# Loading each piece of MLP weights in two transfers of 117 and 11 rows

## The chip, the cores and the metric

The kernel runs on one core of a Trainium2 chip. The core has TensorE (matrix multiplications), VectorE, ScalarE and GpSimd (element-wise work), SyncE (which here only issues DMAs), and 16 DMA engines that move data between HBM and the on-chip memory SBUF. The metric is the device time of one execution in microseconds; the profile's "span" is the part of it from the first to the last instruction of the program.

## What is computed

A recurrence over 768 time steps (RWKV-7, for 4 batches of 8 heads with 40 channels), whose output of 3072 tokens x 320 channels goes through an MLP with a hidden width of 2048.

```python
    for t in range(S):
        kt, vt, rt = (k[:, :, t], v[:, :, t], r[:, :, t])
        wt, at, bt = (w[:, :, t], a[:, :, t], b[:, :, t])
        y[:, :, t] = np.einsum('bhd,bhde->bhe', rt, state)
        Sa = np.einsum('bhde,bhe->bhd', state, at)
        state_decay = state * wt[:, :, None, :] - np.einsum('bhd,bhe->bhde', Sa, bt)
        state = state_decay + np.einsum('bhd,bhe->bhde', vt, kt)
...
    h = x @ w_in
    g = h * (1.0 / (1.0 + np.exp(-1.702 * h)))
    return (g @ w_out).astype(np.float32)
```

The weights w_in (320 x 2048) and w_out (2048 x 320) come as 64-bit floating-point numbers, since the setup scales them by a 64-bit factor. The kernel turns them into 32-bit numbers on the chip.

## The kernel before

**Tiling.** The sequence is cut into 12 chunks of 64 steps, and each chunk into two units of two batches, 24 units in all. For a unit, `load_w` and `load` fetch its inputs (logw, wc, ak, b, rv, RV, time), `decay` and `prep` scale them, `inverse` inverts a triangular system in five "levels" (TensorE into `ps_level`, copies by ScalarE and VectorE, transposes into `EX`), and `solve` applies the state and writes the unit's output `x`. `part_with` and `get_back` (lines 979 to 989) write x to DRAM and read it back transposed, as `xT`. After every second unit, `mlp` adds the chunk's matmuls into `ps_up` and `ps_down` (lines 995 to 1044). The recurrence hands its state from unit to unit; the MLP only needs its chunk's xT and the weights.

**Order of the work.** Nothing is scheduled by the compiler. Every piece of work is a task with a rank, a cost for each engine that may run it, and the tasks it comes after. `Plan.order` (line 105) simulates the engines with these costs and writes out one order of instructions; `refined` (line 247) shifts ranks at random and keeps what its own simulation calls shorter. Each engine then runs its instructions strictly in that order, and semaphores join the engines. SyncE is one such queue: a DMA that waits there holds up all those behind it. The DMAs share eight semaphores in turn, so that each DMA also waits until the one eight places before it has landed.

**The weights.** They are kept in one tile `w_sb` for the whole kernel. `weights` (line 505) loads them in eight pieces, four of w_in and four of w_out, of 128 rows x 1280 numbers of 64 bits, or 1280 KB. Each piece goes through `weight` (line 462): one DMA (line 498) puts the 64-bit numbers in a place that is free at the time (the spare tile `extra`, a part of `w_sb` that is not filled yet, or the buffers of `xT`, as the list `raws` says). Then ScalarE takes the upper words (`rebased`, line 478), VectorE clamps and shifts them (482, 486) and scales the lower words (490), and GpSimd adds the two (`joined`, 494). In the order that results, the first five pieces are issued between 12.9 and 17 us of the span, the sixth at 41.0, the seventh at 65.7 and the eighth at 94.2 us.

**The other DMAs.** Loads of ak, b and rv come in two DMAs of 40 rows each (line 528); logw, wc, RV and time in one of 128 rows; x goes out in two of 40 rows and comes back in two of 64; results go out in two of 64.

## Time and profile before

| | |
|---|---|
| median of 3 runs | 716.97 us (716.28 to 717.66) |
| the profiled execution | 715.64 us, span 713.9 us |
| TensorE clock granted, mean | 0.985 |
| DMA traffic | 69.81 MB in 31,860 packets, mean 98 GB/s |
| of it instruction fetches | 159 packets on q8, 21 on q14 |
| TensorE busy 12 to 50 us | 26.0 of 38 us, clock 0.78, DMA engines busy 0.88 |
| TensorE busy 50 to 80 us | 22.3 of 30 us, clock 0.93, DMA engines busy 0.53 |
| TensorE busy 80 to 110 us | 28.3 of 30 us, clock 1.00, DMA engines busy 0.36 |
| TensorE busy 110 to 714 us | 593.4 of 604 us, clock 1.00, DMA engines busy 0.27 |

The last four rows are stretches of the span. DMA engines busy is the mean over the 16 engines. In a time line each row gives the start in us from the span's beginning, the duration, engine, line, operation and tiles, how many equal instructions follow each other, and in brackets the time that the engine sat idle before it and what ended that. SPq is the queue that issues DMAs; its durations are those of the issuing alone.

### The profile page before, as it was taken

To read this page: it belongs to the slowest core of one execution; us is meant where nothing else is said; L and a number is where in the kernel's file an instruction comes from. 1 tells how busy PE (TensorE), PEld (TensorE's weight loads), DVE (VectorE), ACT (ScalarE), POOL (GpSimd) and SP (SyncE) were. 2 spreads that over 40 slices of the span, in tenths; PEclk is the share of its full clock that TensorE was granted. 3 is DMA by queue.
4 is the path that set the end of the run, shared out by engine and by line. 5 is a ranking of instruction groups with operands and counts; after the bars stand their busy time and mean duration, and the time that the engine had idled before them with its cause. 6 is when DMAs were issued, how large, how long until landed. Compare 5 with 4: busy or idle time off the path is not lost.

```text
span 713.9 us, 43522 instructions
## 1 busy us (share of the span) xinstructions
PE 673.0 (94%) x20256; PEld 562.4 (79%) x20256; DVE 423.8 (59%) x747; ACT 347.7 (49%) x683; POOL 204.6 (29%) x260
## 2 busy tenths in 40 slices
PE   4667899999999999999999999999999999999997
PEld 4566779887888788788888998779978788877563
DVE  6689777756766576577474775666675656421000
ACT  4465636656365465454555565256445535342020
POOL 5367244442431321331342233220341320200000
PEclk9879999999999999999999999999999999999999
DMA  7955351431441341341432241251341230111000
GB/s 244 394 193 181 111 168 47 139 99 44 129 121 32 113 137 32 111 139 42 120 121 86 72 124 50 83 147 33 107 115 32 81 96 5 41 49 31 20 3 19
DMA packets 31860, 69.81 MB, mean 98 GB/s; under 512 B 5056, under 2 KB 14272, under 8 KB 30656
## 3 DMA queue, kind: packets, MB, share of 16 engines
q1 hardware_dynamic: 31680, 67.03, 30.5%
q8 instruction: 159, 2.61, 1.5%
q14 instruction: 21, 0.17, 0.1%
HBM read 59.15 MB, written 7.86 MB: 94 GB/s over the span
## 4 chain that ended last, share of the span: by engine, by line
PE 88%; DVE 5%; issue 3%; DMA 2%; ACT 1%; SPq 0%; ACTq 0%; DVEq 0%
PE ps_down L330 29%; PE ps_up L330 28%; PE ps_level L330 9%; PE ps_y L330 4%; PE ps_B L330 4%; PE ps_X L330 2%; PE ps_T L330 1%; PE ps_Q L330 1%; PE ps_rz L330 1%; PE ps_A L330 1%; PE ps_RV L330 1%; PE ps_N L330 1%; PE ps_zT L330 1%; PE ps_cum L330 1%; DMA rv<-in_rv 1%
## 5 line engine op out<-in xcount | busy, mean ns | idle before, releaser
L330 PE MATMUL ps_up<-xT_all,w_sb 64*64 64x256 f32 x3840 | 251.7, 378 | 1.8 <-issue 1.7
L330 PE MATMUL ps_down<-w_sb,g 64*64 64x320 f32 x3072 | 243.0, 431 | 0.8 <-issue 0.6
L330 PEld LDWEIGHTS ps_up<-xT_all,w_sb 64*64 64x64 f32 x3840 | 157.5, 133 | 27.1 <-issue 2.7
L330 PEld LDWEIGHTS ps_down<-w_sb,g 64*64 64x64 f32 x3072 | 131.1, 133 | 45.4 <-issue 2.4
L736 ACT ACTIVATE EX<-ES,quads 128x256 f32<-128x256 f32 x124 | 56.2, 501 | 56.8 <-DVE ES L731 56.4
L1008 ACT ACTIVATE g<-ps_up 128x1024 f32<-128x1024 f32 x48 | 49.1, 1024 | 39.6 <-PE ps_up L330 39.4
L330 PEld LDWEIGHTS ps_level<-W,EX 64*64 64x64 f32 x2560 | 57.5, 134 | 8.3 <-ACT zT L878 1.0
L780 ACT COPY W<-ps_level 128x512 f32<-128x512 f32 x55 | 32.2, 586 | 55.3 <-PE ps_level L330 54.7
L657 POOL TENSOR_TENSOR kh<-time,G 128x320 f32<-128x320 f32 x23 | 20.9, 910 | 131.9 <-PE ps_y L330 70.7
L330 PE MATMUL ps_level<-W,EX 64*64 64x64 f32 (+1 forms) x2560 | 55.7, 218 | 0.9 <-ACT zT L878 0.6
L782 DVE TENSOR_TENSOR E<-two,ps_level 128x256 f32<-128x256 f32 x80 | 33.2, 415 | 39.1 <-ACT W L780 38.7
L1034 DVE TENSOR_TENSOR ob<-ob,ps_down 128x320 f32<-128x320 f32 x24 | 11.6, 482 | 59.6 <-ACT ob L1032 58.7
L726 POOL TENSOR_TENSOR PT<-two,PT 128x256 f32<-128x256 f32 x18 | 13.1, 728 | 109.8 <-DVE PT L719 105.1
L330 PE MATMUL ps_level<-PT,EX 64*64 64x64 f32 (+2 forms) x1280 | 37.5, 250 | 5.0 <-issue 4.0
L330 PEld LDWEIGHTS ps_level<-PT,EX 64*64 64x64 f32 x1280 | 35.4, 152 | 7.9 <-issue 4.9
L973 POOL TENSOR_TENSOR x<-zr,FT 128x128 f32<-128x128 f32 x80 | 40.9, 539 | 0.0
L731 DVE STREAM_TRANSPOSE ES<-E 128x256 f32<-128x256 f32 x80 | 35.6, 444 | 3.9
L911 ACT COPY B<-ps_B 128x416 f32<-128x416 f32 x38 | 19.1, 504 | 37.2 <-PE ps_B L330 36.9
L330 PE MATMUL ps_y<-RV,kh 64*64 64x104 f32 x768 | 35.7, 251 | 1.4 <-DVE M L927 1.4
L330 PE MATMUL ps_y<-M,bh 64*64 64x104 f32 x768 | 35.6, 249 | 1.2 <-issue 1.2
L649 POOL TENSOR_TENSOR ak<-ak,FT 128x512 f32<-128x512 f32 x16 | 21.5, 1345 | 50.0 <-DMA ak<-in_ak 31.0
L1032 ACT COPY ob<-ps_down 128x320 f32<-128x320 f32 x22 | 9.4, 425 | 53.1 <-PE ps_down L330 53.0
(136 smaller groups left out, 1168.1 us busy)
## 6 DMA issues: line engine op xcount, KB each, us to landing
time<-in_time SPq DMA_DIRECT2D x24, 320.0 KB
ak<-in_ak SPq DMA_DIRECT2D x48, 160.0 KB
rv<-in_rv SPq DMA_DIRECT2D x48, 160.0 KB
xT_all<-x_dram SPq DMA_DIRECT2D x48, 160.0 KB
wc<-in_wc SPq DMA_DIRECT2D x20, 264.0 KB
logw<-in_w SPq DMA_DIRECT2D x24, 160.0 KB
RV<-in_v SPq DMA_DIRECT2D x24, 160.0 KB
b<-in_b SPq DMA_DIRECT2D x48, 80.0 KB
```

The costliest lines, as they stand in the source:

```text
L330: nc.tensor.matmul(o, lhsT, rhs, start=start, stop=True, skip_group_check=True)
L649: plan.add(R, {"DVE": 690.0, "POOL": 1270.0, "sbuf": True}, lambda t: of(t.engine).tensor_mul(ahT(), ahT(), FT_of(i)), reads=T("ak", "FT") ...
L657: plan.add(R + 4, {"POOL": 870.0, "DVE": 490.0, "sbuf": True}, lambda t, n=n, dst=dst: of(t.engine).tensor_mul(dst(i)[:, :, :D], by_head(t ...
L726: plan.add(R, {"DVE": 430.0, "POOL": 750.0, "sbuf": True}, lambda t: of(t.engine).tensor_sub(at(W0_t, i)[:, :, :32], two32.unsqueeze(1).to ...
L731: plan.add(rank, dve(256), lambda t: nc.vector.transpose(ES(n), source(t)), writes=[key("ES", n, 6)], **reads)
L736: nc.scalar.activation(dst[:, :, h], ES(n), ACT.Copy, scale=quads[:, h, :1])
L780: plan.add(rank, any2(512), lambda t: copy(t.engine)(tiles_of(W(n + 1)), blocks(psum(t, ""), 64)), writes=[key("W", n + 1, 5)], pair=pair)
L782: plan.add(rank, dve(256), lambda t: nc.vector.tensor_sub(tiles_of(E(n + 1)), every(two32, [128, 2, 4, 32]), blocks(psum(t, ""), 64)[:, :, ...
L911: plan.add(R, any2(416), lambda t: copy(t.engine)(dst(), psum(t, "")[:, :, :208]), writes=[("Bv", i)] if x and c > 0 else T("B"), pair=(na ...
L973: of(t.engine).tensor_mul(x[:, b ^ u, b], both(i)[:, at, :64], FT_of(i)[:, at])
L1008: plan.add(-45, {"ACT": 1030.0, "table": "gelu"}, lambda t: nc.scalar.activation(g_of(c * NQ + q).rearrange("p m r n -> p r m n"), psum(t, ...
L1034: plan.add(-45, dve(320), lambda t: nc.vector.tensor_add(ob_of(serial), ob_of(serial), psum(t, "")[:, 1, :DM]), reads=[("ob", serial)], wr ...
```

## The change

Each of the eight pieces of weights is loaded by two DMAs in place of one: rows 0 to 116, then rows 117 to 127, into the same places. The planner's task stays one task with the same cost, so the order of tasks on every engine is the same as before. What reads a piece now waits for both DMAs, and the semaphores of all DMAs behind are handed out anew.

```diff
+    ROWS = [slice(0, 117), slice(117, 128)]
...
-        plan.add(rank, {"SP": 350.0}, lambda t: nc.sync.dma_start(raw(), src), reads=before, writes=T("wt"), size=128 * PIECE * 8)
+        def fetched(t):
+            for some in ROWS:
+                nc.sync.dma_start(raw()[some], src[some])
+        plan.add(rank, {"SP": 350.0}, fetched, reads=before, writes=T("wt"), size=128 * PIECE * 8)
```

## The prediction

> **What bounds the kernel now.** I read the page first (busy shares, slices, DMA queues), then the chain of waits for the first 150 us, the list of waits, the time lines of TensorE, ScalarE and the DMA-issuing queue, and at last the trace's own records of single DMA packets, which no view prints.

> ```profile
> PE 673.0 (94%) x20256; PEld 562.4 (79%) x20256; DVE 423.8 (59%) x747; ACT 347.7 (49%) x683; POOL 204.6 (29%) x260
> ...
> PE   4667899999999999999999999999999999999997
> ...
> PEclk9879999999999999999999999999999999999999
> DMA  7955351431441341341432241251341230111000
> ...
> q8 instruction: 159, 2.61, 1.5%
> ```

> TensorE is full from the fifth slice on, so what is to be won lies in the first 80 us or so: 713.9 - 673.0 = 40.9 us of idle TensorE, 28.6 of it (from a table of 5 us stretches) before the first MLP matmul at 79.2 us. In that time the TensorE clock also drops and the DMA engines are at their busiest. The q8 line is the key: 159 packets, 2.61 MB, so 16.4 KB a packet. It is TensorE's program, fetched while it runs.

> What TensorE waits for between 15 and 110 us, and where its time line shows it:

> ```profile
> PE ps_level L330 <- issue: 5.5, 3, 2.4
> PE ps_X L330 <- DVE T L853: 3.3, 2, 2.9
> PE ps_cumc L330 <- issue: 2.1, 1, 2.1
> PE ps_Q L330 <- POOL T L738: 1.9, 1, 1.9
> PE ps_up L330 <- issue: 1.7, 1, 1.7
> PE ps_RV L330 <- issue: 1.3, 1, 1.3
> ```

> ```profile
> 23.13 0.42 PE L330 MATMUL ps_level<-PT,ident 64*64 64x128 f32 x4 [1.55 <-issue]
> ...
> 29.80 0.77 PE L330 MATMUL ps_cumc<-edges,logw 64*64 64x65 f32 x28 [2.10 <-issue]
> ...
> 36.27 0.48 PE L330 MATMUL ps_level<-PT,EX 64*64 64x96 f32 x12 [1.56 <-issue]
> ...
> 68.26 0.45 PE L330 MATMUL ps_RV<-rv 64*64 64x64 f32 x11 [1.33 <-issue]
> ...
> 74.78 1.38 PE L330 MATMUL ps_level<-PT,EX 64*64 64x96 f32 x26 [2.43 <-issue]
> ```

> "issue" is a wait that no semaphore explains. Counted in TensorE's records, each such stop stands exactly where 256 instructions end (records 705, 961, 1217, 3009, 3265 and, at 101.44 us, 4801, all 193 modulo 256), and TensorE goes on 1.2 to 1.6 us after a 16 KB packet of q8 has ended. So these six stops, 1.55 + 2.10 + 1.56 + 1.33 + 2.43 + 1.74 = 10.7 us, are waits for the program. The packet itself takes 0.9 to 1.4 us everywhere; what differs is its start after TensorE enters the block before: mostly 0.1 to 2.1 us, but 3.98, 4.33, 3.76, 3.97 and 4.27 us for blocks entered at 16.9, 23.1, 29.8, 68.3 and 94.9 us. Those are the times at which weights move:

> ```profile
> 12.91 0.33 SPq L498 DMA_DIRECT2D extra<-in_w_in  x1
> 13.40 0.81 SPq L498 DMA_DIRECT2D w_sb<-in_w_in  x2
> ...
> 65.65 0.35 SPq L498 DMA_DIRECT2D extra<-in_w_out  x1
> ...
> 94.15 0.35 SPq L498 DMA_DIRECT2D extra<-in_w_out  x1
> ```

> A piece is 1280 KB, 128 rows of 10,240 bytes; a row takes 0.39 us in the packet records, so 8 rows on each of 16 engines are 3.1 us, just the delay of a fetch. The fetch stands behind the weights' share of one DMA engine.

> The chain of waits (start, us, what) holds five of the six; the one at 66.8 us is not on it:

> ```profile
> 21.58 1.55 issue
> ...
> 72.35 2.43 issue
> ...
> 99.71 1.74 issue
> ```

> [...]packets of the 40-row loads (4,096 bytes) run ten at a time and hardly ever more.[...]

> **The change part by part.**
> (1) Eight more DMAs on the sync queue, 0.35 us each to issue. Every DMA there waits for the landing of the one eight places earlier, so the halves use up places: unit 2's b (issued at 17.6 and 20.7 us) will wait for the third piece, unit 2's ak (27.8) for the fourth, its second half of rv (32.5) for the fifth. With the slower pieces below I get about 28, 32 to 34 and 37 us. First uses are at 45.5 (POOL, ak), 47.2 (VectorE, b) and 52.4 us (TensorE, rv): covered by 8 us or more, also if the work comes 4 us sooner. Cost 0; without that cover up to 3 us.

> (2) A piece takes 10 rows x 0.39 = 3.9 us[...] instead of 3.1. The first five pieces ended at 19.4, 22.7, 26.1, 30.1 and 35.4 us; each falls 0.8 us further behind: about 20.3, 24.3, 28.5, 33.3 and 39. Their readers on ScalarE:

> ```profile
> 20.68 1.39 ACT L478 ACTIVATE w_sb<-extra 128x1280 f32<-128x1280 f32 x1
> 26.28 0.80 ACT L813 COPY PT<-ps_level 128x768 f32<-128x768 f32 x1 [4.21 <-PE ps_level L330]
> ```

> The first piece is read at once, so ScalarE will stand about 0.9 us with the copy of ps_level queued behind it, but it sits 4.2 us before that copy anyway. The others are read at 35.0, 36.4, 38.7 and 45.6 us, 5 us or more after landing, except the fifth if the work moves up by more than 5 us. Cost 0, at worst 2. The sixth and later pieces lose a tail instead: in the eighth, one engine ran on alone from 100.9 to 102.8 us, and ScalarE waited 1.0 us for it.

> (3) [...]If the fetch queue lies on one of them, a fetch starts about 1 us after its block is entered, lands 3.4 us after it (1.1 + 1.0 + 1.3), and nearly every block before 80 us takes TensorE longer than that. Which engine it is the trace does not print. It shows one thing: in the fetch at 234.1 us (0.94 us long) packets of 4,096 bytes fill 9.6 us, ten whole engines, so the fetch is on none of those ten[...].[...]I take 0.69 for a free one.

> What the stops are then worth, by what is late next. First stop: the next level needs VectorE's EX, ready at 22.3 us, against 24.1 when it began: 1.5 of 1.55. Second: the level at 30.44 needs EX ready at 29.3: 1.1 of 2.10. Third: needs EX ready at 35.6, begun at 36.8: 1.2 of 1.56. The chain then runs through VectorE's weight conversions to 46 us, which follow from TensorE's results and move with it. Sum 3.8. Fourth (1.33): VectorE is busy 5.00 of 5 us from 60 to 70 us and carries the chain: 0. Fifth (2.43): next late is x, written at 68.6 us to DRAM[...] behind the seventh piece, read back by the DMAs at 74.8 and 75.3 us, and needed by the first MLP matmul at 79.2; that piece is now 0.8 us longer there. I take 0.5, between 0 and 2.4. Sixth (1.74): TensorE is the bound, and what follows waits 0.3 us at most: 1.4. Together 3.8 + 0.5 + 1.4 = 5.7 us.

> (4) Extra semaphore waits on ScalarE and VectorE: eight more[...], beside idle time: 0.

> The profiled run has a span of 713.9 us (715.64 with what lies around it) against a median of 716.97 us for the three runs shown. 713.9 - 5.7 = 708.2; on the median 711.3 us. After 80 us TensorE has no slack to lose, so what is gained there is kept to the end.

> **The rivals.**
> Forecast, 0.48: 4 to 8 us gained, 709 to 713.
> More, 0.08: half-clock stretches of 3.4 us begin at 23.3, 30.2 and 74.5 us, each just after a stop. If they go with it, up to 1.7 us each: 8 to 12 us in all, 705 to 709. Against: TensorE is only 60 to 70% busy there anyhow.
> Gain given back, 0.13: fetches run free, but the weights or x are late next.[...] If a piece took 5.2 us (a third over 3.9, a guess), the fifth would land near 44 us, after the (earlier) time at which ScalarE wants it, with all later ScalarE work queued behind: 4 to 6 us back, 715.5 to 718.
> Slower, 0.27: [...]a fetch waits for 9 or 10 rows, not 8: 0.4 to 0.8 us more on each of six stops, 2 to 4 us on the chain, with x up to 0.8 us later: 718.5 to 721.5. It decides if fetches in the weight stretch still start 4 us after their block.
> Not what it says, 0.04: 117 rows land on far fewer engines; a piece on one engine would be 117 x 0.39 = 46 us, and the time over 740. Against: the ten engines of the 40-row loads.

> **How the numbers follow.** A difference under 0.2% (1.4 us) cannot be told from none here. Faster: 0.48 + 0.08 = 0.56; same 0.13; slower 0.27 + 0.04 = 0.31. The range 705 to 720.5 takes in the forecast and the third case, most of the second and over half of the fourth, some 0.83. The likeliest case alone is 709 to 713.

> **What would show it.** Right: the issue waits at 23, 30 and 36 us gone, ps_level's issue time from 5.5 us to under 1, first ps_up near 75 us, sixth stop gone. Step 2 wrong: ScalarE waits for weights by over 1 us apiece. Step 1 wrong: loads of units 2 and 3 ending waits at 45 to 55 us. Forecast wrong altogether: the same six stops, a little longer.

## The result: 2.8% slower, and the profile after

The changed kernel took 737.83 us (median of 4 runs, 735.07 to 739.91) against 717.32 us for the kernel before on the same chip (716.28 to 719.37): ratio 1.028, 95% interval 1.0239 to 1.0321. The profiled execution took 739.91 us with a span of 738.2. The forecast was 711.3 us in a range of 705 to 720.5; the kernel got slower instead of faster. Of the kernels below, runs 3 and 7 were profiled in a slow execution (755.28 and 738.32 us, where their fastest took 740.22 and 725.44 us), so their row times and waits come from it, while their ratios leave it out.

The page of the changed kernel: busy time, the slices, a DMA queue and the engines of the chain that ended last.

```profile
PE 675.1 (91%) x20256; PEld 561.7 (76%) x20256; DVE 423.2 (57%) x747; ACT 347.6 (47%) x683; POOL 204.5 (28%) x260
...
PE   4452788999999999999999999999999999999997
...
PEclk9867799999999999999999999999999999999999
DMA  7877435243153152252332331441331230110000
...
q1 hardware_dynamic: 31744, 67.03, 32.2%
...
PE 80%; DMA 10%; issue 3%; POOL 2%; DVE 2%; ACT 2%; SPq 0%; ACTq 0%; POOLq 0%; DVEq 0%
```

TensorE's busy time has hardly changed (673.0 before, 675.1 after); the span has grown by 24.3 us, so 22.2 us of it are idle TensorE. Most of them lie at the start: TensorE reaches 9 tenths in the eighth slice, before in the sixth, and slices three and four have fallen from 6 and 7 tenths to 5 and 2. The same bytes keep the DMA engines busy for longer: q1's share is 32.2% of a longer span (30.5% before). Of the chain that ended last, DMAs are now 10%, before 2%.

The stretches of the changed kernel, cut as in the table of before (columns: stretch, length, busy us of TensorE, its weight loads, VectorE, ScalarE and GpSimd with instructions, TensorE's clock, busy share of the DMA engines, GB/s):

```profile
12.00:50.00 38.00, 20.39 (x714) 18.30 (x709) 22.89 (x32) 16.45 (x35) 12.44 (x8) 0.85 0.87 225
50.00:80.00 30.00, 15.23 (x520) 13.68 (x516) 14.16 (x18) 10.98 (x29) 11.40 (x10) 0.68 0.60 173
80.00:110.00 30.00, 24.48 (x837) 21.76 (x833) 25.70 (x35) 16.16 (x31) 13.26 (x10) 0.94 0.43 132
110.00:739.00 629.00, 612.69 (x18163) 505.75 (x18152) 351.96 (x652) 298.77 (x574) 158.88 (x188) 1.00 0.28 79
```

Between 12 and 110 us TensorE has done 60.1 us of work, 76.6 before. Over the first 140 us it is 89.19 against 109.63 us, so by then TensorE is 20.4 us of work behind, most of the 24.3 us by which the span has grown. The same stretch from 15 to 50 us in both kernels, first before, then changed:

```profile
15.00:50.00 35.00, 23.01 (x700) 21.05 (x696) 24.25 (x34) 18.99 (x38) 15.95 (x10) 0.77 0.87 326
15.00:50.00 35.00, 17.39 (x598) 15.30 (x590) 20.90 (x29) 16.08 (x34) 12.44 (x8) 0.83 0.85 221
```

The DMA engines are as busy as before (0.85 against 0.87), but they move 221 GB/s where they moved 326. They are not short of work; each packet takes longer.

ScalarE's readers of weights in the time line of the changed kernel:

```profile
26.36 1.38 ACT L479 ACTIVATE w_sb<-extra 128x1280 f32<-128x1280 f32 x1 [5.59 <-DMA extra<-in_w_in]
39.69 2.64 ACT L479 ACTIVATE w_sb<-w_sb 128x1280 f32<-128x1280 f32 x2
47.54 1.36 ACT L479 ACTIVATE w_sb<-extra 128x1280 f32<-128x1280 f32 x1 [4.21 <-DMA extra<-in_w_in]
53.55 1.37 ACT L479 ACTIVATE w_sb<-xT_all 128x1280 f32<-128x1280 f32 x1 [3.59 <-DMA xT_all<-in_w_out]
72.81 1.35 ACT L479 ACTIVATE w_sb<-extra 128x1280 f32<-128x1280 f32 x1 [10.11 <-DMA extra<-in_w_out]
92.20 1.41 ACT L479 ACTIVATE w_sb<-extra 128x1280 f32<-128x1280 f32 x1 [1.29 <-DMA extra<-in_w_out]
126.13 1.35 ACT L479 ACTIVATE w_sb<-extra 128x1280 f32<-128x1280 f32 x1 [4.58 <-DMA extra<-in_w_out]
```

The bracketed waits add up to 29.4 us; before, the waits for arriving weights were 0.69 + 1.01 = 1.7 us (a third, of 1.66 us, was ended by GpSimd). Everything queued on ScalarE behind such a read stands too, and TensorE with it. What TensorE waits for most between 15 and 110 us (us in total, times, longest), and the two long stops of its time line that no semaphore explains (two more last 0.4 us each):

```profile
PE ps_T L331 <- ACT QT L844: 13.2, 2, 9.3
PE ps_cumc L331 <- issue: 5.0, 1, 5.0
PE ps_level L331 <- issue: 3.6, 1, 3.6
PE ps_Q L331 <- POOL T L742: 2.5, 1, 2.5
PE ps_level L331 <- DVE EX L756: 2.2, 4, 0.9
```

```profile
25.17 0.48 PE L331 MATMUL ps_level<-PT,ident 64*64 64x128 f32 x3 [3.64 <-issue]
...
34.46 0.74 PE L331 MATMUL ps_cumc<-edges,logw 64*64 64x65 f32 x28 [5.02 <-issue]
```

QT is a copy by ScalarE that stands in its queue close behind a read of weights: 13.2 us of TensorE's time, and nothing of the kind before. Where six fetch stops made up 10.7 us before, two long ones now make up 8.7 us. The chain that ended last (start, us, what) says the same; the list holds only pieces of it that are DMAs, and the read of weights behind the last:

```profile
13.33 12.59 DMA extra<-in_w_in
...
25.95 21.51 DMA extra<-in_w_in
...
54.08 4.57 DMA rv<-in_rv
...
113.93 12.11 DMA extra<-in_w_out
...
126.13 1.35 ACT w_sb L479
```

In the packet records, which no view prints, one row of 10,240 bytes took 388 ns before (median; mean 427) and takes 569 ns after (mean 593). Between 15 and 53 us thirteen packets of weights run at a time in 37% of the time in which any do, and more than thirteen in 5%, as the change meant (before, up to 35 us, sixteen in 33% and more in 4%). The rows of the first five pieces moved from 15.0 to 35.4 us before and from 15.1 to 53.0 us after: 37.9 us in place of 20.4. These figures are not fixed: three more executions with the same rows 117 and 11, and the planner as it was (runs 14, 15 and 16), had medians of 514, 425 and 579 ns and 32.1, 29.7 and 39.4 us. All are above before.

### The profile page after: what moved, and what is told of

It reads as the page before. It is cut to its first block, busy times and chain, and to the rows that moved or that the text cites. A ratio compares the mean times of both kernels' runs of the same rounds, so it can differ in the third digit from the quotient of the medians.

```text
span 738.2 us, 43537 instructions
## 1 busy us (share of the span) xinstructions
PE 675.1 (91%) x20256; PEld 561.7 (76%) x20256; DVE 423.2 (57%) x747; ACT 347.6 (47%) x683; POOL 204.5 (28%) x260
## 2 busy tenths in 40 slices
DMA packets 31925, 69.82 MB, mean 95 GB/s; under 512 B 5120, under 2 KB 14336, under 8 KB 30720
## 3 DMA queue, kind: packets, MB, share of 16 engines
q1 hardware_dynamic: 31744, 67.03, 32.2%
q8 instruction: 159, 2.61, 1.5%
## 4 chain that ended last, share of the span: by engine, by line
PE 80%; DMA 10%; issue 3%; POOL 2%; DVE 2%; ACT 2%; SPq 0%; ACTq 0%; POOLq 0%; DVEq 0%
PE ps_down L331 27%; PE ps_up L331 26%; PE ps_level L331 7%; DMA extra<-in_w_in 5%; PE ps_y L331 4%; PE ps_B L331 4%; PE ps_X L331 2%; DMA extra<-in_w_out 2%; PE ps_T L331 2%; PE ps_rz L331 1%; DMA ak<-in_ak 1%; PE ps_Q L331 1%; PE ps_A L331 1%; PE ps_N L331 1%; PE ps_zT L331 1%
## 5 line engine op out<-in xcount | busy, mean ns | idle before, releaser
L331 PE MATMUL ps_up<-xT_all,w_sb 64*64 64x256 f32 x3840 | 254.7, 378 | 1.7 <-ACT PT L817 1.4
L331 PEld LDWEIGHTS ps_up<-xT_all,w_sb 64*64 64x64 f32 x3840 | 159.1, 133 | 28.4 <-issue 1.7
L331 PEld LDWEIGHTS ps_down<-w_sb,g 64*64 64x64 f32 x3072 | 131.5, 133 | 47.2 <-issue 4.1
L331 PE MATMUL ps_level<-PT,EX 64*64 64x64 f32 (+2 forms) x1280 | 35.5, 245 | 6.0 <-ACT g L1012 3.2
L977 POOL TENSOR_TENSOR x<-zr,FT 128x128 f32<-128x128 f32 x80 | 40.9, 540 | 0.0
L331 PEld LDWEIGHTS ps_level<-PT,EX 64*64 64x64 f32 x1280 | 33.7, 148 | 9.0 <-ACT g L1012 3.7
L735 DVE STREAM_TRANSPOSE ES<-E 128x256 f32<-128x256 f32 x80 | 35.6, 444 | 4.3 <-DVE E L786 0.5
L331 PE MATMUL ps_y<-RV,kh 64*64 64x104 f32 x768 | 35.6, 250 | 2.0 <-DVE M L931 2.0
L915 ACT COPY B<-ps_B 128x416 f32<-128x416 f32 x38 | 19.2, 504 | 37.1 <-PE ps_B L331 36.8
L331 PE MATMUL ps_y<-M,bh 64*64 64x104 f32 x768 | 35.6, 249 | 0.6 <-issue 0.6
```

Source lines behind the costliest of these rows:

```text
L331: nc.tensor.matmul(o, lhsT, rhs, start=start, stop=True, skip_group_check=True)
L735: plan.add(rank, dve(256), lambda t: nc.vector.transpose(ES(n), source(t)), writes=[key("ES", n, 6)], **reads)
L915: plan.add(R, any2(416), lambda t: copy(t.engine)(dst(), psum(t, "")[:, :, :208]), writes=[("Bv", i)] if x and c > 0 else T("B"), pair=(na ...
L977: of(t.engine).tensor_mul(x[:, b ^ u, b], both(i)[:, at, :64], FT_of(i)[:, at])
```

## The experiments

Times are ratios to the kernel before on the same chip, with 95% intervals where there were several rounds; for a kernel that was run once, its single time is given beside that of the kernel before. "Late" means the time from the start of a fetch's block on TensorE to the first packet of the next block, from the packet records. "Stands" of ScalarE are its waits for weights between 10 and 140 us.

**1. Halves of the rows.** Are thirteen engines too few, do two DMAs cost something, or is a row slow in a split transfer however many engines are at work?

```diff
-    ROWS = [slice(0, 117), slice(117, 128)]
+    ROWS = [slice(0, 64), slice(64, 128)]
```

> Rows 0 to 63 and 64 to 127: two DMAs a piece as in the change[...].[...] Fewer engines (13 instead of 16, 10 rows instead of 8 cause the loss): a row takes 0.39 us, a piece 3.5 us, time 715 to 720 us. Two DMAs (the places among the eight semaphores cause it): rows of 0.39 us, time 725 us or more.

Measured: 1.0314 (1.0274 to 1.0355). A row took 768 ns, twice the 388 of before, and five pieces took 37 us. There were no fewer rows at a time: 640 rows of 768 ns in 37 us make 13.3, an estimate, as 640 of 388 ns in 20.4 us make 12.2 before and 640 of 569 ns in 37.9 us make 9.6 in the changed kernel. In run 11, with the same rows, the busy share of the DMA engines between 20 and 40 us was 1.02, so all sixteen were at work (0.92 before, 0.84 in the changed kernel). TensorE's waits between 10 and 140 us:

```profile
PE ps_level L331 <- issue: 14.9, 5, 5.0
PE ps_cumc L331 <- issue: 5.3, 1, 5.3
PE ps_RV L331 <- issue: 5.2, 2, 4.1
```

Each fetch stop is now up to 5.3 us, and the fetches were 6.5 to 7.0 us late (3.8 to 4.3 before). So the loss comes without fewer engines too.

**2. Two DMAs of all 128 rows and half the columns.**

```diff
-    ROWS = [slice(0, 117), slice(117, 128)]
+    COLS = [slice(0, PIECE // 2), slice(PIECE // 2, PIECE)]
...
-            for some in ROWS:
-                nc.sync.dma_start(raw()[some], src[some])
+            for some in COLS:
+                nc.sync.dma_start(raw()[:, some], src[:, some])
```

> Each piece in two DMAs of all 128 rows and half the columns: [...]packets of 5,120 bytes. Two DMAs (places among the eight semaphores, issue time): slower than before by 5 us or more. [...]fewer engines: packets of 0.20 us, a piece 3.5 us, time within 3 us of before. Fetch depth (a fetch stands behind some eight descriptors that an engine has taken in, not behind the whole share): fetches under weights start 2.5 to 3 us after their block instead of 4, and the time is 1 to 4 us below before.

Measured: 1.0009 (0.9986 to 1.0032). Half a row took 196 ns, and five pieces moved from 15.6 to 37.1 us. Eight DMAs more, with their issue time, semaphores and the window of eight places, cost nothing that can be told from the noise as long as the pieces keep their speed. ScalarE waits 1.3 us for arriving weights (and 1.7 us once in front of a read of weights, put down to a load of ak):

```profile
ACT w_sb L479 <- DMA extra<-in_w_out: 1.3, 2, 0.9
```

The fetches were 3.2, 4.0 and 4.3 us late, as before, though half the columns also halve a DMA's share of an engine (8 x 0.196 = 1.6 us, an estimate from sixteen packets at a time as before): these fetches waited for more of the queue of weights than one DMA's share.

**3. More engines freed: rows 100, 20 and 8.**

```diff
-    ROWS = [slice(0, 117), slice(117, 128)]
+    ROWS = [slice(0, 100), slice(100, 120), slice(120, 128)]
```

> Rows 0 to 99, 100 to 119, 120 to 127[...]. [...]fetches under weights start about 1 us after their block and the issue waits of TensorE go; if they still start 4 us or more after it, the fetch queue [...]waits for something other than its engine.[...] Fewer engines[...]: rows of 0.39 us, a piece about 5 us, time 725 to 735 us.

Measured: 1.0413 (1.0364 to 1.0461). In the first burst the fetches were 0.9, 0.5, 0.7 and 0.5 us late and no stop over 0.2 us was left between 10 and 140 us; a row took 606 ns, five pieces 47.4 us, and ScalarE stood 49 us. That more engines are free is shown by run 10, with the same rows: the busy share of the DMA engines between 20 and 40 us was 0.68, in the changed kernel 0.84. So this split does help the fetches, and what they save is much less than what slow pieces cost. The row of 0.39 us of "fewer engines" did not come true.

**4. Smaller packets.** The kernel before with packets of 2,560 bytes, one DMA of 128 rows (the copy in HBM is laid out in four blocks of columns).

```diff
...
-        plan.add(rank, {"SP": 350.0}, lambda t: nc.sync.dma_start(raw(), src), reads=before, writes=T("wt"), size=128 * PIECE * 8)
+        plan.add(rank, {"SP": 350.0}, lambda t: nc.sync.dma_start(raw().rearrange("p (q n) -> p q n", q=4), src.rearrange("q p n -> p q n")), reads=before, writes=T("wt"), size=128 * PIECE * 8)
...
-        return np.ascontiguousarray(x.reshape(4, 128, 1280)).view(np.int64)
+        return np.ascontiguousarray(x.reshape(4, 128, 4, 320).transpose(0, 2, 1, 3)).view(np.int64)
```

> The kernel before, with each piece still in one DMA of 128 rows, but laid out in DRAM in four blocks of columns, so that a descriptor moves 2,560 bytes instead of 10,240. Fetch depth (a fetch waits for some eight descriptors): fetches under weights start about 1.9 us after their block instead of 4, the six issue waits of 1.3 to 2.4 us mostly go, and the time is 3 to 7 us below before. Fetch behind the whole share of the engine: fetches as before, time within 1.5 us of before.[...]

Measured: 1.001 (0.9987 to 1.0033), fetches 3.7 to 4.2 us late as before. That a fetch waits for a fixed number of packets is out.

**5 and 6. Rows 108 and 20; rows 110 and 18.** These were meant to free more engines than the change does. The edit of run 5; run 6 has 110 in place of 108.

```diff
-    ROWS = [slice(0, 117), slice(117, 128)]
+    ROWS = [slice(0, 108), slice(108, 128)]
```

> Rows 0 to 107 and 108 to 127[...]. [...]the fetches of the blocks entered between 15 and 45 us start about 1 us after their block and no issue wait is left; [...]they start 4 us or more after it.[...]

> Rows 0 to 109 and 110 to 127[...]. [...]fetches start about 1 us after their block between 15 and 45 us, no issue wait; [...]4 us or more, issue waits of 3 us or more.[...]

Measured, one execution each: 735.7 and 748.04 us, before 716.75; rows of 476 and 664 ns. With rows 108 and 20 the first fetch of the burst was 5.1 us late and the next three 1.8, 1.2 and 0.9, which none of the cases on record had. With 110 and 18 all four came within 1.3 us, and the busy share of the DMA engines between 15 and 50 us was 0.74 (0.85 in the changed kernel); how many engines each of the two leaves free is not shown. I read this at first as one fixed engine. Runs 14 to 16 show that this reading was wrong. ScalarE in the time line of the second kernel:

```profile
25.78 1.35 ACT L479 ACTIVATE w_sb<-extra 128x1280 f32<-128x1280 f32 x1 [7.03 <-DMA extra<-in_w_in]
...
41.89 1.35 ACT L479 ACTIVATE w_sb<-w_sb 128x1280 f32<-128x1280 f32 x1 [6.35 <-DMA w_sb<-in_w_in]
50.36 1.35 ACT L479 ACTIVATE w_sb<-extra 128x1280 f32<-128x1280 f32 x1 [6.13 <-DMA extra<-in_w_in]
57.95 1.36 ACT L479 ACTIVATE w_sb<-xT_all 128x1280 f32<-128x1280 f32 x1 [5.18 <-DMA xT_all<-in_w_out]
76.76 1.35 ACT L479 ACTIVATE w_sb<-extra 128x1280 f32<-128x1280 f32 x1 [9.49 <-DMA extra<-in_w_out]
```

With a single fetch stop of 0.4 us up to 140 us, this execution is slower than any of the changed kernel, for ScalarE stands about 44 us here (the list leaves out three shorter waits).

**7. Rows 112 and 16**, meant to keep all engines at work.

> Rows 0 to 111 and 112 to 127[...]. Fewer engines as the cause of the loss: a row takes 0.39 us, a piece 3.5 us, time within 3 us of before. [...]the first five end near 42 us instead of 35 (before) and 53 (the change), and the time lies between the two, 720 to 732 us. Fetches wait 4 us or more.

Measured: 1.0188 (1.013 to 1.0246). A row took 706 ns, five pieces 14.9 to 51.5 us. Again slow rows, and again no fewer at a time than before (640 of 706 ns in 36.6 us make 12.3, an estimate): "fewer engines as the cause", with its row of 0.39 us and a time within 3 us of before, did not come true. The ratio lies within the other case's 720 to 732 us (1.005 to 1.021), though the five pieces ended far behind its 42 us.

**8. The changed kernel with a planner that knows of longer pieces.**

```diff
-        plan.add(rank, {"SP": 350.0}, fetched, reads=before, writes=T("wt"), size=128 * PIECE * 8)
+        plan.add(rank, {"SP": 350.0}, fetched, reads=before, writes=T("wt"), size=int(1.75 * 128 * PIECE * 8))
```

> The change, but the planner is told that a piece takes 1.75 times as long, as measured, so that it puts the readers of the weights later in the order of ScalarE and VectorE. Order (the loss comes from ScalarE standing in its fixed order before weights that are late, with the recurrence's copies behind them): most of the loss comes back, 717 to 728 us, and ScalarE waits for weights 5 us or less in all instead of 29. Transfers (late weights or late inputs hold up the work wherever their readers stand): 733 us or more.

Measured: 1.0237 (1.0185 to 1.029). ScalarE stood 0.8 us, as meant, but the time can't be told from the changed kernel's 1.028; of the two cases on record, "transfers" came true and "order" did not. TensorE's longer stops in the time line:

```profile
25.16 0.47 PE L331 MATMUL ps_level<-PT,ident 64*64 64x128 f32 x3 [4.21 <-issue]
33.36 1.08 PE L331 MATMUL ps_level<-PT,EX 64*64 64x96 f32 x20 [3.88 <-issue]
53.27 0.97 PE L331 MATMUL ps_B<-RV,A 64*64 64x104 f32 x16 [1.61 <-issue]
67.74 0.33 PE L331 MATMUL ps_y<-M,bh 64*64 64x104 f32 x1 [5.01 <-issue]
```

The fetches are late all the same, and the first ps_up comes at 102.7 us (97.4 in the changed kernel, 79.2 before). The planned order changes where the loss falls; here it did not remove it.

**9 and 10. Both mended: many free engines and a planner that is told.** Run 9 has rows 110 and 18, run 10 rows 100, 20 and 8. Both kernels were told 2.15 times the length (the text on record says 2.2 for the first). The planner also models fetches that wait beside a large transfer; for these two that wait was set to zero, as fetches on free engines were thought to come at once.

```diff
-    BESIDE, LARGE, BESIDE_LARGE = 0.35, 1e6, 0.63
+    BESIDE, LARGE, BESIDE_LARGE = 0.35, 1e6, 0.0
...
-    ROWS = [slice(0, 117), slice(117, 128)]
+    ROWS = [slice(0, 110), slice(110, 128)]
...
-        plan.add(rank, {"SP": 350.0}, fetched, reads=before, writes=T("wt"), size=128 * PIECE * 8)
+        plan.add(rank, {"SP": 350.0}, fetched, reads=before, writes=T("wt"), size=int(2.15 * 128 * PIECE * 8))
```

> Rows 0 to 109 and 110 to 127 ([...]TensorE's fetches should come within 1.3 us and without issue stops, as with the planner unaware), and the planner told a piece that takes 2.2 times as long, so that ScalarE should hardly stand for weights. This is the change as it was meant, as nearly as these row splits allow. Theory 'both costs, then the later order': with both kinds of stop gone, what is left is that pieces of 9 us instead of 3.5 put the weights and the inputs behind them 15 to 30 us later, and TensorE must fill that time with other work; ratio to before 1.00 to 1.02, no issue stops over 1 us before 70 us, stands of ScalarE for weights under 3 us in all. Rival 'the forecast gain is there once ScalarE doesn't stand': under 0.995. Rival 'nothing but the length of the pieces counts, whoever waits': as with the planner unaware, 1.035 or more.

> The same with rows 0 to 99, 100 to 119 and 120 to 127 and a piece told as 2.15 times as long: [...]it repeats the test with another set of rows. Theory 'both costs, then the later order': ratio 1.00 to 1.02, beside 1.041 with the planner unaware. Rival 'the forecast gain is there': under 0.995. Rival 'only the length counts': 1.035 or more.

Measured: 1.0341 (1.0296 to 1.0386) and 1.033 (1.0291 to 1.037). My theory (1.00 to 1.02) failed, and so did the forecast's gain; the ratios lie just under the 1.035 of "only the length counts", between it and the theory. Against the same rows with the planner not told, 1.033 stands beside run 3's 1.0413, and 1.0341 beside 1.044 for the one execution of run 6, so some of the loss may come back. ScalarE stood under 3 us, but the fetches were not all prompt: 3.7 and 3.2 us late near 12 us, 5.5 and 5.8 us near 18 us, and more after 47 us. Free engines (between 20 and 40 us the busy share of the DMA engines was 0.73 and 0.68, in the changed kernel 0.84) were plainly not enough for them, and the planner's zero was wrong, so these two do not show what prompt fetches and a told planner would give together; that stays open.

**11. Halves again, with another order of the rows in HBM.**

```diff
-    ROWS = [slice(0, 117), slice(117, 128)]
+    ROWS = [slice(0, 64), slice(64, 128)]
...
-                nc.sync.dma_start(raw()[some], src[some])
+                nc.sync.dma_start(raw()[some], src.rearrange("(p h) n -> h p n", h=2)[some.start // 64])
...
+        x = x.reshape(4, 2, 64, 1280).transpose(0, 2, 1, 3)
```

> Rows 0 to 63 and 64 to 127 as in the run with halves, but the DRAM copy holds the rows of the two halves alternately, so that each row is read at another distance from its neighbours (two rows apart instead of one)[...]. [...]the row stays at 0.77 us (0.74 to 0.79), the piece at about 7 us, and the ratio at 1.025 to 1.037. Rival 'the DRAM side': the row moves by more than 0.05 us in either direction, and the time with it.

Measured: row 786 ns, ratio 1.0366 (1.0298 to 1.0433). Twice the distance between the rows in HBM changed the row by 18 ns (768 in run 1), so that distance is not the cause. What else sets a row in a split transfer apart, no run tested.

**12 to 14. Which engine serves a fetch?** The changed kernel's first four fetches in the burst were 5.3 and 6.3 us late, then 1.1 and 0.8, with weights on their way all the time. No single engine that was free or busy throughout explains that. Run 12 adds 128 small products (run 13: 256) near the start:

```diff
             ps = psum(t, "ps_N")
+            for _ in range(128 if i == 0 else 0):
+                mm(ps[HALF[0], 0, 256:257], ident[HALF[0]], ident[HALF[0], :1], True)
```

> The changed kernel with 128 small matrix products more (and their 128 weight loads, so 256 instructions, as many as lie between two fetches) on TensorE in its idle time from 5.4 to 11.4 us. Each later point of the program is then served by the fetch with the next number. Theory 'each fetch goes to the next DMA engine in turn': in the changed kernel the fetches at 17.2 and 25.2 us [...]were 5.3 and 6.3 us late, and the next two[...] took 1.1 and 0.8 us; now [...]only the first is late (over 4 us, one stop of 3 to 5 us), and the second and third come within 1.8 us. Rival 'one fixed engine, and the moment decides': two late ones and then two prompt ones, as before.

> The same with 256 products and 256 loads more, two fetches' worth (some 9 us of TensorE, 6 of them in its idle time, so what follows may be up to 3 us later). Theory 'in turn': [...]the first two come within 1.8 us and no issue stop over 1 us falls into the first 35 us; the fourth is late if pieces are still on their way. Rival 'fixed engine': the first two are 4 to 7 us late with stops of 3 to 5 us each.

> The changed kernel once more, so that it is seen whether the order of late and prompt fetches is that of the program or of the single execution. Both theories as stated: if the turn starts at the same engine in each execution, the fetches at about 17 and 25 us are over 4 us late and the next two under 1.8 us, as in the first profile; if the turn starts elsewhere each time, the late ones are at other numbers.

The first two told nothing. Each product is carried out in two passes (the trace has 512 more TensorE instructions, not 256, so two fetches more, and four in the second), and a pass took 107 ns, so 27.4 us in all for run 12, so that other work met the burst: 740.3 and 768.43 us. The repeat of the changed kernel (731.56 us) was useful: 4.4, 6.3, 1.1 and 1.2 us late, the same pattern as in the first profile.

**15 and 16. More fetches, long after the burst.**

Run 15 puts 64 of the same products into the thirteenth unit, run 16 puts 128 there.

```diff
+            for _ in range(64 if i == 12 else 0):
+                mm(ps[HALF[0], 0, 256:257], ident[HALF[0]], ident[HALF[0], :1], True)
```

> The changed kernel with 64 small products more in the middle of the run (first matrix of the thirteenth unit, long after the burst of weights): 256 instructions on TensorE and so one fetch more in all, 160 instead of 159; everything up to the thirteenth unit is the same program. The products take some 7 us where they stand, so the total says nothing here. Theory 'each fetch goes to the next DMA engine in turn, and the turn goes on from one execution to the next': the engines of the first fetches move by one for each execution that came before, so the late and prompt ones at about 17, 25, 34 and 39 us (late, late, prompt, prompt in both profiles of the changed kernel) change their pattern; with one execution before, late, prompt, prompt, late. Rival 'the turn starts at the same engine each time' and rival 'one fixed engine': late, late, prompt, prompt, as in the changed kernel.

> The same with 128 products, 512 instructions and two fetches more in all. Theory 'the turn goes on from one execution to the next': the pattern moves twice as far; with one execution before, prompt, prompt, late, late. Rivals 'starts at the same engine' and 'one fixed engine': late, late, prompt, prompt.

| | fetches in an execution | how late the four fetches of the first burst were, us |
|---|---|---|
| changed kernel | 159 | 5.3, 6.3, 1.1, 0.8 |
| the same again | 159 | 4.4, 6.3, 1.1, 1.2 |
| 64 products later on | 160 | 3.6, 1.8, 1.7, 4.5 |
| 128 products later on | 161 | 1.2, 0.9, 5.9, 5.8 |

The program up to the end of the burst is the same in all four, and the pattern moves by just one place for each fetch added after it: late, late, prompt, prompt; late, prompt, prompt, late; prompt, prompt, late, late. Both rivals said it would stay. The stops in TensorE's time line between 20 and 80 us, with 64 products and then with 128:

```profile
22.56 0.38 PE L331 MATMUL ps_level<-PT,ident 64*64 64x128 f32 x4 [1.71 <-issue]
27.20 0.63 PE L331 MATMUL ps_cumc<-edges,logw 64*64 64x65 f32 x28 [1.30 <-issue]
38.52 0.70 PE L331 MATMUL ps_level<-PT,ident 64*64 64x128 f32 x8 [1.58 <-issue]
53.99 0.69 PE L331 MATMUL ps_A<-ak 64*64 64x64 f32 x32 [3.21 <-issue]
```

```profile
24.41 0.69 PE L331 MATMUL ps_cumc<-edges,logw 64*64 64x65 f32 x31 [0.26 <-issue]
33.08 0.75 PE L331 MATMUL ps_level<-PT,EX 64*64 64x96 f32 x12 [2.00 <-issue]
```

The stops of 3.6 and 5.0 us are gone from their places; the fetch stops that are left last 0.3 to 2.0 us and stand elsewhere. The 3.21 us at 54 us do not stand at the end of a block of 256 instructions, so they are no fetch stop. The totals, 741.29 and 758.84 us, hold the products themselves and say nothing. This is what a turn predicts: each fetch goes one step further than the one before, and the turn goes on from one execution to the next. Each of these kernels was run once, but both shifts were on record beforehand, and the repeat shows that the pattern does not change by chance alone. At least four fetches in a row are prompt with rows 110 and 18 (run 6), three with 108 and 20 (run 5), two with 117 and 11; why just so many, and why one fetch of run 10 was late in the first burst while run 3, with the same rows, had none there, stays open. That the steps are DMA engines is inferred, for no record names a fetch's engine.

## Why the prediction was wrong

**Step 2 failed, and with it the forecast.** The term that failed is the duration of a row. The step says "A piece takes 10 rows x 0.39 = 3.9 us", and took the row's 0.39 us over from 128-row transfers. The number of rows fits: thirteen packets at a time make 128 / 13 = 9.8. The row does not: 569 ns, and five pieces ended at about 53 us where the step had 39. Ten rows for eight make 1.25 times, as the step had it, and a row of 569 ns for 388 makes another 1.47; the five pieces took 37.9 / 20.4 = 1.86 times as long. It put ScalarE's stand for the first piece at 0.9 us and the whole step at 0, at worst 2; measured were 5.59 for the first and 29.4 in all.

Run 2 clears the second DMA as such of blame, runs 1 and 7 have the slow row (768 and 706 ns) with no fewer rows at a time than before (13.3 and 12.3 against 12.2, estimates), and run 11 clears the distance of the rows in HBM. In the profiled executions with the planner not told (runs 3 and 7 left out), the time follows the five pieces: 21.5 us and 1.000 times before (columns), 32.1 and 1.021 (run 14), 37.1 and 1.029 (halves), 37.9 and 1.031 (the change), 42.1 and 1.044 (110 and 18); 38.2 and 1.026 (108 and 20) and 40.2 and 1.033 (run 11) lie a little lower. So the slow row is shown to be what the forecast missed.

Why it is slow is not shown. The row of 388 ns is that of the 128-row transfers alone, halves of the rows take twice as long, and the same rows, 117 and 11, took 425 ns in one execution and 579 in another; no record names a packet's engine, and no run here tells what makes the difference.

**Step 3 failed twice.** "Which engine it is" was the wrong question: by runs 14 to 16 no place in the program has a fixed one, so free engines, three with thirteen packets at a time on sixteen, seem to help only those fetches whose turn falls on them, two of four in the first burst. The other two met slower rows (569 ns against 388) and were later than before (5.3 and 6.3 us against 4.0 and 4.3). The stops still make up 8.7 of 10.7 us. And where all four fetches were prompt (runs 3 and 6), the 5.7 us of gain did not appear; ScalarE stood 49 and 44 us there. The argument from the ten engines of the 40-row loads looked at one fetch alone; under a turn one fetch says nothing of the next. Nor need it be weights that a fetch waits for: in the changed kernel the fetch for the block entered at 406.1 us was 3.75 us late, without a stop, long after the last weights had landed at 125.6 us (in the kernel before, none of those after its last weights was over 2.5 us late). That in the burst it is the weights is shown by runs 3 and 6, where nothing but another split of the weights' rows made the same fetches prompt (at most 0.9 and 1.3 us late).

**Step 1** was right that the eight DMAs cost nothing in themselves (run 2), and wrong about what the window of eight places does with slow pieces: unit 2's b, ak and second half of rv were put at about 28, 32 to 34 and 37 us; b was issued from 39.3 us, ak from 46.6, the pair of rv from 48.3 to 53.5, and the rv issued behind them at 54.1 is on the chain. The sign that the prediction named for a failure of this step, loads that end waits at 45 to 55 us, came true as well, if in part a little later (GpSimd took up this ak at 45.53 us before, without a wait; the wait of VectorE's line for b is put down to a load of rv):

```profile
54.63 0.69 DVE L655 SCALAR_TENSOR_TENSOR b<-b,GT 128x512 f32<-128x512 f32 x1 [2.98 <-DMA rv<-in_rv]
56.81 1.86 POOL L653 TENSOR_TENSOR ak<-ak,FT 128x512 f32<-128x512 f32 x1 [7.73 <-DMA ak<-in_ak]
```

**Step 4**, no cost of more semaphore waits: run 2, which adds as many, shows none that can be told from the noise.

**The rivals.** "Gain given back" came nearest: it has slow pieces, weights that land too late and ScalarE's later work queued behind them. Its piece was 5.2 us "(a third over 3.9, a guess)". The five pieces took 37.9 / 5 = 7.6 us each. At that size it does not give 4 to 6 us back but costs 20. "Slower" had the sign right, but by luck: it had fetches wait for nine or ten rows, which at 569 ns make 5.1 to 5.7 us, an estimate near the 5.3 and 6.3 us of the two late ones, but two such stops (8.7 us) do not outweigh the six of before (10.7); the loss came by way of the weights. The test named for step 2, waits of ScalarE for weights of over 1 us apiece, was one that came true, six times.

Two readings of the profile in the prediction were loose, without weight for the result: the fifth slice of TensorE is 8 tenths busy and only the sixth 9, and the half-clock stretch at 74.5 us begins within the stop that ends at 74.78 us, not after it.

## What to carry to other kernels

The duration of a row depended on the shape of the transfer, and not only on its bytes (388 ns in transfers of 128 rows, 425 to 786 in split ones): before a transfer is split by rows, look up in the packet records what a row takes in a transfer of that very shape, in more than one execution, or split it by columns, which cost nothing here that can be told from the noise (1.0009). Freeing a resource is worth only what those save who are served by it, here two of four fetches in the first burst; the other two were later than before. Where a planner's order is kept, late data stops a whole engine queue (ScalarE stood 29.4 us); where the planner was told, the loss moved and for the most part stayed: no kernel with a row split had a ratio under 1.018.
